# Half of x0 by a casting DMA, gated weights, x5 to x7 transposed by DMA, and state weights on 128x32 tiles in a fused attention and token-mixing kernel

## The chip, the cores and the metric

The kernel runs on one core of one Trainium2 chip. The metric is the device time of one execution in microseconds (us), lower is better. Executions fall into a fast and a slow state (of the changed kernel's five runs, 92.04 to 92.69 us against 93.85 and 94.79); all comparisons below are of fast runs, and where a profile was taken in a slow run this is said. The engines are PE (TensorE, matmuls), PEld (its weight loads), DVE (VectorE), ACT (ScalarE), POOL (GpSimd) and SP (here only a DMA issuer).

## The reference

Two layers. The first is a cross attention both ways between x (8 batches, 8 heads, 512 tokens, 64 values) and a state of 32 rows per head; the second mixes tokens with weights made from the tokens themselves.

```python
def _attn_ref(x, state):                       # x: 8,8,512,64; state: 8,8,32,64
    scores = scale * x @ state.T               # softmax, then xread = a @ state
    scores2 = scale * state @ x.T              # softmax, then sread = a2 @ x
    return np.concatenate([xread, sread], axis=2)
# ... heads are joined: 8, 544, 512
def _moe_ref(x, w_q, w_k, w_out):
    wq, wk = x @ w_q, x @ w_k                  # 64 wide
    W_tok = scale * np.einsum('bsd,btd->bst', wq, wk)
    mixed = np.einsum('bst,btd->bsd', W_tok, x)
    return np.maximum(mixed, 0) @ w_out
```

## The kernel before

One string, ORDER, lists every step as name.batch.form; a loop issues them in that order, and the trace has each engine's own in it (ACT: xc1.0 at 4.25 us, stf.0 at 6.00, xTe0.0 at 8.34). Forms: "t" is a matmul over the whole 128x128 array, "c" splits the output rows in two 64-column tiles (twice the instructions), a/v/p name ACT, DVE or POOL, "r" marks a step of fixed form. The data comes in as f32, and PE works in bf16. Batch 0 is loaded as f32 and cast on the engines; the others are cast by the DMA that POOL issues.

```python
ORDER = """
zst.0.p ix1.0.p stc.0.v xc1.0.a fill.1.t stt.0.c ste.0.v stbd.0.p stf.0.a xc0.0.p xc3.0.v ix2.0.p
fill.7.t xT0.0.t xc2.0.v xTe0.0.a fill.1.t xT1.0.t is.0.p ...
"""                                             # ... cut
    st_load(0, 1)                               # state of batch 0, f32, SP
    for g in range(4):                          # x0 in four f32 loads
        eng = nc.sync if g % 2 == 0 else nc.scalar
        eng.dma_start(out=x_f0[:, 2 * g : 2 * g + 2], in_=xsrc(0, 2 * g, 2 * g + 2))
    st_load(1, 3)
    for t in range(2):                          # w_q, w_k: four loads, no gate
        for r in range(2):
            nc.sync.dma_start(out=w_f[64 * r : 64 * r + 64, :, t, :], in_=wsrc[t][r])
    # ...
    def fill(n, b, e):                          # dummy matmuls that keep PE busy
        ps = psA.tile([128, 512], FP, name="fill_ps", tag="psA")
        for w in range(b):
            nc.tensor.matmul(out=ps, lhsT=zero[:, 0:128], rhs=zero, start=True, stop=True)
    def load(n, b, e):                          # ix1..ix7: f32 to bf16 by DMA
        nc.gpsimd.dma_start(out=x_bf[b], in_=xsrc(b, 0, H))          # cut
    def zeros(n, b, e):
        nc.gpsimd.memset(stT.bitcast(FP), 0.0)
    def sw_mm(n, p, e):                         # state weights: state @ w_q, w_k
        # for bb, q, r:
        nc.tensor.matmul(out=ps[NS * q : NS * q + NS, r, ...],
            lhsT=stT[64 * r : 64 * r + 64, 2 * p + bb, r, NP * r + q, :],
            rhs=w_qk[64 * r : 64 * r + 64, q, 0:2, :], start=True, stop=True)
    def xT_mm(n, b, e):                         # half a batch of x transposed on PE
        for q in range(NP):
            for u in range(2):
                tr(e, ps[:, u, q, :], x_bf[b][:, NP * r + q, 128 * u : 128 * u + 128])
    def x_dT(n, b, e):                          # defined, not used before
        xT = work.tile([128, H, 2, 128], BF, name="xTd", bufs=3)
        nc.sync.dma_start(out=xT.rearrange("p h u t -> p (h u) t"),
            in_=x_bf[b].rearrange("p h f -> p (h f)"), transpose=True)
        for r in range(2):
            L[b][f"xTe{r}"] = xT[:, NP * r : NP * r + NP].rearrange("p q u t -> p u q t")
```

Of each batch the steps are: xT (transpose x), pt (scores), exp, sums and srd (state read), wq/wk/g/v (small products), mix, fin (output product with w_out), os (store). fs and fix are the last output products.

The softmax here doesn't subtract the row's maximum and nothing guards it: scores larger than these inputs give would overflow.

## Time and profile before

| before | value |
|---|---|
| time, median of the runs beside the changed kernel | 88.26 us (87.6 to 88.69) |
| span of the profiled run, mean granted clock | 87.0 us, 0.991 |
| packets under 512 B, of all packets | 3712 of 15119 |
| x transposes on PE | 16 half batches |

How to read it: a page gives each engine's busy share, a row of tenths of busy time for 40 slices, the DMA queues and the chain of work that ended last. The prediction below shows those parts. Here are lines that it does not show: the DMA queues of the page (packets, MB, share of the 16 engines' span), then the view of the weights' tile, and two lines of the timeline (start us, length us, what).

```profile
q1 hardware_dynamic: 4880, 8.98, 28.0%
...
q8 instruction: 12, 0.20, 0.9%
```

```profile
L123 SPq DMA_DIRECT2D w_f<-in_moe_w_k_dram x2: 595/605/615, 4.2 to 4.9; - x2
L142 ACT CAST w_qk<-w_f x1: 620/620/620, 11.1 to 11.1; 128x512 bf16<-128x512 f32 x1
...
DMA to landing us min/median/max: 4.8/5.8/6.4
```

```profile
1.25 1.80 POOL L201 MEMSET stT<- 128x2048 f32 x1
...
3.67 0.41 DVE L144 CAST st_bf<-st_f 128x128 bf16<-128x128 f32 x1 [2.07 <-DMA st_f<-in_state_dram]
```

To see there: the weights are issued by 4.9 us and cast at 11.1, well ahead of their first use at 13.7 us. POOL's memset of stT is over (1.25 + 1.80) before DVE's first cast starts.

### The profile page before, as it was taken

How to read it: one execution, taken by the hardware profiler on the slowest of the kernel's cores; microseconds unless marked ns; L12 is line 12 of the kernel's file. 1: busy time of each engine (PE TensorE's matmuls, PEld its weight loads, DVE VectorE, ACT ScalarE, POOL GpSimd, SP SyncE). 2: the span in 40 equal slices, each digit the busy share in tenths (PEclk: the TensorE clock that was granted, in tenths of full speed). 3: DMA queues.
4: the chain of work that ended last, by engine and by line, in shares of the span. 5: the costliest groups of instructions: out<-in, count | busy, mean ns of one | idle time of the engine just before them, and what ended most of it. 6: DMA issues, size and time to landing. Idle time of an engine off the chain costs nothing.

```text
span 87.0 us, 3553 instructions
## 1 busy us (share of the span) xinstructions
PE 80.8 (93%) x1572; PEld 53.4 (61%) x1579; DVE 52.4 (60%) x111; ACT 55.9 (64%) x83; POOL 45.1 (52%) x58
## 2 busy tenths in 40 slices
PE   4999999999999999999999999999999999999910
PEld 1326666878777778777689747866755565544400
DVE  2125793997956875897856957891688264056010
ACT  1541637999898858778797838967930592665530
POOL 7999948999999969408507735327150000000000
PEclk9999999999999999999999999999999999999996
DMA  0899999999609999995600464201461663566782
GB/s 12 292 312 187 202 191 198 195 165 147 96 0 121 143 128 277 322 169 72 241 8 4 171 281 175 115 8 53 188 243 45 275 281 136 213 269 277 294 314 80
DMA packets 15119, 15.00 MB, mean 172 GB/s; under 512 B 3712, under 2 KB 12672, under 8 KB 15104
## 3 DMA queue, kind: packets, MB, share of 16 engines
q0 software_dynamic: 9104, 4.36, 39.7%
q1 hardware_dynamic: 4880, 8.98, 28.0%
q10 hardware_dynamic: 1120, 1.44, 4.6%
q8 instruction: 12, 0.20, 0.9%
q14 instruction: 3, 0.02, 0.1%
HBM read 10.22 MB, written 8.91 MB: 220 GB/s over the span
## 4 chain that ended last, share of the span: by engine, by line
PE 90%; ACT 4%; issue 1%; DVE 1%
PE fin_ps L161 20%; PE fin_ps L163 12%; PE fill_ps L155 6%; PE xT_ps L174 5%; PE mix_ps L541 5%; PE warm_ps L132 4%; PE srd_ps L369 3%; PE xT_ps L170 3%; PE at_ps L174 3%; PE v_ps L505 3%; PE pt_ps L163 2%; PE g_ps L163 2%; PE fins_ps L163 2%; PE wq_ps L433 2%; PE v_ps L514 2%; PE wk_ps L163 2%
## 5 line engine op out<-in xcount | busy, mean ns | idle before, releaser
L346 POOL TENSOR_TENSOR A<-E,rinv 128x1024 bf16<-128x1024 bf16 (+1 forms) x9 | 15.4, 1717 | 12.8 <-DVE rinv L340 12.5
L161 PE MATMUL fin_ps<-w_o,rmix 128*64 128x512 bf16 x160 | 19.4, 380 | 0.0
L142 ACT COPY ost<-fin_ps 128x1024 f32<-128x1024 f32 (+2 forms) x13 | 11.2, 864 | 11.6 <-PE fin_ps L161 5.9
L148 ACT ACTIVATE rmix<-mix_ps 128x1024 bf16<-128x1024 f32 x12 | 12.1, 1024 | 2.4 <-PE mix_ps L541 2.4
L407 POOL TENSOR_TENSOR sbd<-srn,mask 128x256 bf16<-128x256 bf16 x16 | 9.4, 614 | 6.0 <-DVE srn L397 5.9
L144 DVE COPY ost<-fin_ps 128x1024 f32<-128x1024 f32 (+1 forms) x6 | 6.5, 1091 | 9.9 <-PE fin_ps L163 5.4
L161 PEld LDWEIGHTS <-rmix 128*64 128x64 bf16 x160 | 8.4, 110 | 6.2 <-issue 0.6
L332 DVE TENSOR_REDUCE rsum<-E 128x16 f32<-128x512 bf16 x16 | 10.8, 676 | 0.9 <-ACT E L317 0.6
L163 PE MATMUL fin_ps<-w_o,rmix 128*128 128x512 bf16 x44 | 11.0, 379 | 0.2
L317 ACT ACTIVATE E<-pt_ps 128x512 bf16<-128x512 f32 x16 | 9.5, 601 | 2.5 <-PE pt_ps L161 1.3
L142 ACT COPY xT<-xT_ps 128x1024 bf16<-128x1024 bf16 x7 | 7.1, 1012 | 4.6 <-PE xT_ps L174 3.9
L234 POOL TENSOR_TENSOR stbd<-st_bf,mask 128x256 bf16<-128x256 bf16 x16 | 9.3, 610 | 0.4 <-DVE st_bf L144 0.2
L155 PE MATMUL fill_ps<-zero 128*128 128x512 bf16 x21 | 7.8, 432 | 0.1
L144 DVE COPY xT<-xT_ps 128x1024 bf16<-128x1024 bf16 x9 | 6.2, 690 | 2.7 <-PE xT_ps L174 2.5
L150 DVE TENSOR_SCALAR rmix<-mix_ps 128x1024 bf16<-128x1024 f32 x4 | 4.9, 1222 | 3.4 <-PE mix_ps L541 3.4
L163 PEld LDWEIGHTS <-rmix 128*128 128x128 bf16 x48 | 4.3, 98 | 4.0 <-ACT rmix L148 0.2
L183 POOL DMA_DIRECT2D x_bf<-in_x_dram x7 | 6.6, 949 | 0.0
L174 PE MATMUL xT_ps<-ident,x_bf 128*128 128x128 bf16 x80 | 6.0, 219 | 0.2 <-ACT E L317 0.2
L174 PEld LDWEIGHTS <-x_bf 128*128 128x128 bf16 x80 | 5.1, 98 | 1.3 <-issue 0.5
L541 PE MATMUL mix_ps<-wq,V 64*128 64x256 bf16 x64 | 5.8, 272 | 0.0
L132 PE MATMUL warm_ps<-zero 128*128 128x512 bf16 x8 | 3.6, 631 | 1.2 <-DVE mask L133 1.2
L163 PE MATMUL pt_ps<-stT,xT 128*128 128x64 bf16 x88 | 4.4, 193 | 0.0
(90 smaller groups left out, 139.7 us busy)
## 6 DMA issues: line engine op xcount, KB each, us to landing
out_dram<-ost SPq DMA_DIRECT2D x14, 512.0 KB, 2.8
x_bf<-in_x_dram POOLq DMA_DIRECT2D x7, 512.0 KB, 7.8
out_dram<-ost ACTq DMA_DIRECT2D x3, 256.0 KB, 2.1
x_f<-in_x_dram ACTq DMA_DIRECT2D x2, 256.0 KB, 4.0
x_f<-in_x_dram SPq DMA_DIRECT2D x2, 256.0 KB, 4.4
w_o<-in_moe_w_out_dram POOLq DMA_DIRECT2D x1, 512.0 KB, 8.4
out_dram<-ost SPq DMA_DIRECT2D x2, 256.0 KB, 2.4
st_bf<-in_state_dram POOLq DMA_DIRECT2D x1, 160.0 KB, 7.8
```

Source lines behind the costliest of these rows:

```text
L142: nc.scalar.copy(out=out, in_=in_)
L144: nc.vector.tensor_copy(out=out, in_=in_)
L148: nc.scalar.activation(out=out, in_=in_, func=AF.Relu)
L155: nc.tensor.matmul(out=ps, lhsT=zero[:, 0:128], rhs=zero, start=True, stop=True)
L161: nc.tensor.matmul(out=out[64 * h : 64 * h + 64], lhsT=lh, rhs=rhs, **kw)
L163: nc.tensor.matmul(out=out, lhsT=lhsT, rhs=rhs, **kw)
L174: nc.tensor.transpose(out=out, in_=in_, identity=ident)
L317: nc.scalar.activation(out=L[b]["E"][:, r].rearrange("p c q n -> p c (q n)"), in_=L[b][f"pt{r}"], func=AF.Exp, scale=float(scale),)
L332: nc.vector.reduce_sum(out=L[b]["rsum"][:, w], in_=L[b]["E"].rearrange("p r c q n -> p (r c q) n")[:, w], axis=AX.X,)
L346: eng.tensor_tensor(out=L[b]["A"].rearrange("p r c q n -> p (r c q) n")[:, w], in0=L[b]["E"].rearrange("p r c q n -> p (r c q) n")[:, w], ...
L407: nc.gpsimd.tensor_tensor(out=L[b]["sbd"][:, r], in0=L[b]["srn"][:, r : r + 1, :].to_broadcast((128, NP, D)), in1=mask[:, :, None].to_broa ...
L541: nc.tensor.matmul(out=ps[:, h, kk, :], lhsT=L[b]["V"][rows, 128 * k : 128 * k + 128], rhs=L[b]["wq"][rows, 0:SH], start=True, stop=True,)
```

## The change

The intent: take work off PE, the full engine. Batches 5, 6 and 7 are transposed by a DMA (xs steps, issued on SP; DMA_TRANSPOSE in the trace, called crossbar transposes here). Half of x0 comes in by a casting DMA that is issued first on POOL, and the weight loads wait for the first state cast (the gate: two tiny memsets of w_f on DVE stand behind that cast, at 5.26 us in the trace of after, and the loads follow them at 5.37; before, they began at 2.77). The state weights use the whole 128 rows of the array on 32-column tiles, against zero rows in stT. The whole order of steps is new, with fewer fills.

```diff
-zst.0.p ix1.0.p stc.0.v xc1.0.a fill.1.t stt.0.c ste.0.v stbd.0.p stf.0.a xc0.0.p xc3.0.v ix2.0.p
-fill.7.t xT0.0.t xc2.0.v xTe0.0.a fill.1.t xT1.0.t is.0.p stc.1.v fill.1.t stt.1.c xTe1.0.v stbd.2.p
+ix1.0.p zst.0.p stc.0.v wl.0.v fill.1.t stt.0.c xc1.0.v ste.0.a stf.0.v stbd.0.p xc0.0.v ix2.0.p
+fill.5.t xT0.0.t fill.1.t xT1.0.t xTe0.0.v is.0.p xTe1.0.v fill.1.t pt0.0.t ix3.0.p exp0.0.a stc.1.v
 ... (cut; from further on:)
+rs.4.v wq.2.c wks.2.c wqe.2.a wk.2.t fin3.0.t rinv.4.v wke.2.a xs.5.s srn.3.v A.4.p g.2.t ve.1.v
+sbd.3.p ate.3.v xs.6.s wq.4.c oe0.1.a wks.4.c stbd.6.p wq.3.c wqe.4.v wks.3.c mix1.2.r wqe.3.a
+wke.3.v fin2.1.t exp1.5.a ge.4.v mxe0.2.v g.3.t sums.5.t srd.5.r fin3.1.c srn.5.v os1.0.s xs.7.s
-    x_f0 = const.tile([128, H, NC * D], FP, name="x_f0")
+    x_f0 = const.tile([128, 4, NC * D], FP, name="x_f0")
-    for g in range(4):
-        eng = nc.sync if g % 2 == 0 else nc.scalar
+    for g, eng in enumerate((nc.sync, nc.scalar)):
-    for t in range(2):
-        for r in range(2):
-            nc.sync.dma_start(out=w_f[64 * r : 64 * r + 64, :, t, :], in_=wsrc[t][r])
+    nc.gpsimd.dma_start(out=x_bf[0][:, 4:H], in_=xsrc(0, 4, H))
+    nc.vector.memset(stT[:, 0].bitcast(FP), 0.0)
     def zeros(n, b, e):
-        nc.gpsimd.memset(stT.bitcast(FP), 0.0)
+        nc.gpsimd.memset(stT[:, 1:B].bitcast(FP), 0.0)
+    def w_load(n, b, e):                        # step wl, after the first state cast
+        nc.vector.memset(w_f[:, 0, 0, 0:1], 0.0)
+        nc.vector.memset(w_f[:, 0, 1, 0:1], 0.0)
+        for t in range(2):
+            for r in range(2):
+                nc.sync.dma_start(out=w_f[64 * r : 64 * r + 64, :, t, :], in_=wsrc[t][r])
-                        lhsT=stT[64 * r : 64 * r + 64, 2 * p + bb, r, NP * r + q, :],
-                        rhs=w_qk[64 * r : 64 * r + 64, q, 0:2, :],
+                        lhsT=stT[:, 2 * p + bb, r, NP * r + q, :],
+                        rhs=w_qk[:, q, 0:2, :],
```

## The prediction

> **What bounds the kernel now.** I read three views of the kernel before. First the page: which engine is full, and whether it has holes.

> ```profile
> span 87.0 us, 3553 instructions
> ...
> PE 80.8 (93%) x1572; PEld 53.4 (61%) x1579; DVE 52.4 (60%) x111; ACT 55.9 (64%) x83; POOL 45.1 (52%) x58
> ...
> PE   4999999999999999999999999999999999999910
> ```

> TensorE is busy from the second slice to the last but two with no hole; no other engine passes 64%. A busy PE is not a PE at its peak, so I went next to the chain of waits that ended last, in order of time (start us, length us, what). There one group follows another at the rate at which TensorE takes them in.

> ```profile
> 4.79 0.43 PE fill_ps L155
> ...
> 5.57 2.29 PE fill_ps L155 x7
> ...
> 8.31 0.22 PE fill_ps L155
> ...
> 13.63 1.01 ACT xT L142
> 14.65 0.60 ACT E L317
> ...
> 19.27 0.24 PE sw_ps L246 x16
> 19.51 0.34 PE pt_ps L163 x8
> ...
> 41.00 0.33 PE mix_ps L541 x4
> 41.33 0.98 PE fin_ps L161 x8
> 42.31 0.45 PE xT_ps L170 x16
> 42.76 0.86 PE fin_ps L161 x8
> 43.62 0.25 PE pt_ps L161 x16
> ...
> 79.42 3.47 PE fin_ps L163 x16
> 82.92 0.44 DVE ost L144
> ```

> The reader is to see four things. The chain is almost all PE (90% of the span); the stretches where ACT carries it lie between 13.6 and 18.6 us. A set of transposes of one half batch of x costs 0.45 us of pure PE time (42.31). The same eight fin matmuls cost 0.98 us right after mix and 0.86 us after transposes with an equal tile: changing the tile of the array costs 0.12 us. The same shows at pt (0.34 after sw, where eight of them otherwise take 0.23), and at v and wq (0.34 against 0.22). I take 0.11 per change. Fills are dummy matmuls, 0.43 us on the cold clock and 0.22 us on the warm one. Last, the time from the final matmul (82.9) to the end of the span (87.0) is 4.1 us of eviction, store and finish, which the change does not touch.

> The third view is the DMA issues with their time to landing, because the change moves work there.

> ```profile
> x_bf<-in_x_dram POOLq DMA_DIRECT2D x7, 512.0 KB, 7.8
> ```

> A 512 KB load by casting DMA takes a median 7.8 us to land beside other traffic (5.7 to 10.0 by the view of that tile). The four weight loads take 4.8 to 6.4 us.

> [...]

> **The change part by part.** I counted tiles and changes of tile from the order of the steps in both kernels.

> 1. Transposes of x5, x6, x7 leave TensorE: six half batches (16 before, 10 after) x 0.45 = 2.7 us, all of it on the bounding engine. Their six PSUM copies leave too: three on ACT at 1.01 us and three on DVE at 0.69 us by the grouped rows. Those engines are not the bound, so this is slack only.
> 2. Fills: 23 before, 20 after, two of the three in the group ahead of the first transposes. 3 x 0.22 = 0.65 us. [...]
> 3. Changes of tile, from the new order and the new state weights together: 58 before, 46 after. 12 x 0.11 = 1.3 us. Almost all of it is the order: the new order with the old 64x32 tile would have 47. Only the last sw now sits beside srd, which has the same 128x32 tile.
> 4. State weights on 128x32 tiles: 16 matmuls of 128 columns. Before, they took 0.24 us less a change of 0.11, so 0.13 on eight tiles. With four tiles, 16/4 x 0.056 (one 128-column pass: 0.45 us over 8 transposes) = 0.22. That loses 0.1 x 4 = 0.4 us. [...] one memset of 128x256 on DVE comes in, early and hidden.
> 5. x0 and weights: two of the four f32 loads and two of the four casts go (ACT 0.62, POOL 0.61 us); one casting DMA is issued first on POOL. The first transposes wait in fact for fills (they start at 7.70, while the casts for them ended by 5.9), so the earlier data is worth only what step 2 counts. The weight loads start after the first state cast (3.67 + 0.41 = 4.1) instead of 2.8. Issued 0.6 us apart, the last leaves SP at about 6.2 and lands about 6 later, near 12.3. The cast before was at 11.1, so ACT may wait 1 us there; sw.0 needs it at about 13.4 by my count, so it is just hidden.

> Sum: 2.7 + 0.65 + 1.3 - 0.4 = 4.25 us.

> Given back, as estimates: 0.3 us at the start, because both first xT copies now sit on DVE one behind the other (2 x 0.69) while the chain to pt shrank by a fill; and 0.5 us at the end, where mix, its two evictions and three small relus now stand close together ahead of the last stage with only 0.86 us of fs to cover them. Net 3.5 us. 88.2 - 3.5 = 84.7.

> **The rivals.** (a) DMA transposes land late and TensorE waits for them at pt. Adding up POOL's queue, I get x5 issued near 23, landed near 31, and its pt due near 40; x6 landed near 36, due near 45; x7 landed near 42, due near 51. So each has about 9 us[...]. At 12 us for one, the first pt waits 3 us and the time is near 87.5. Against this: the lead is large, the later two would shift with the first, and the DMA row in that part of the page has holes (31% mean share from 40 to 60 us). [...] (b) ACT or DVE becomes the bound. Against it: both lose some 2 to 4 us of work. I give it little. (c) Start-up takes the gain: late weights or a late casting DMA leave TensorE waiting at 8 to 14 us. That would be 1 to 1.5 us, so 86. (d) The tile change is cheaper than I take it, or the 12 removed are ones that waits hid anyway: then 1.3 falls to about 0.5 and the time is 85.5.

> **Range and chances.** All four terms whole and nothing given back is 84.0; a little more if idle in the ACT-carried stretch (13.6 to 18.6) shrinks too, 83.2. Rivals (c) and (d) together end near 86.5. So 84.7, range 83.2 to 86.8. The 2% mark is 86.46. Faster by over 2%: 0.82; within 2%: 0.14; slower: 0.04.

> **What would show it.** Right: span near 83.5; xT groups on PE 40% fewer; the last matmul near 79.4; no wait of PE for a transposing DMA[...]; DVE and ACT lower; sw groups at about 0.22. Wrong: a hole in the PE row between 38 and 52 us (rival a); holes in the first 15 us with ACT waiting for w_f or PE for x_bf (c); a tail from fs to the end longer by over 1 us; or fin groups still at 0.98 as often as before (d).

## The result, and the profile after

The changed kernel took 92.69 us (median of 5 runs, 92.04 to 94.79; fast ones 92.04, 92.44, 92.69) against 88.26 us: it is slower. The ratio of fast runs is 1.0473, 95% interval 1.0395 to 1.0551. A ratio here is always the mean time of one kernel's fast runs over the mean of the other's fast runs of the same rounds, so it is not quite the ratio of the medians. The predicted range ended at 86.8 us.

The profile of after fell in a slow run (93.85 us, clock 0.990); a fast run of it, profiled later (g0 below), has holes in the same places, smaller, and a longer wait at the start:

```profile
PE sw_ps L250 <- ACT w_qk L139: 1.9, 1, 1.9
...
PE wq_ps L437 <- issue: 0.9, 1, 0.9
PE pt_ps L160 <- DMA xTd<-x_bf: 0.8, 1, 0.8
PE srd_ps L373 <- issue: 0.7, 1, 0.7
```

So the sizes of the single waits below are those of one slow run, and only their places are seen in g0 too. First the page of that run:

```profile
span 90.4 us, 3407 instructions
...
PE 78.5 (87%) x1508; PEld 51.8 (57%) x1508; DVE 52.1 (58%) x110; ACT 51.2 (57%) x75; POOL 45.2 (50%) x58
...
PE   4999993989999999962884999999999999979920
...
q1 hardware_dynamic: 10848, 10.29, 43.8%
```

PE lost 2.3 us of busy time (the prediction counted 4.25), yet the span grew by 3.4. The PE row, solid before, has a dent in slice 7 (13.6 to 15.8 us), a wide one in slices 18 to 22 (38 to 50 us) and a small one ahead of the tail. SP's queue sends 10848 packets and not 4880: the three transposes, three times 2048 packets of 256 B. The chain that ended last, from first to last, by its lines around the dents:

```profile
3.72 1.60 DVE st_bf L141
...
7.49 6.76 DMA w_f<-in_moe_w_k_dram
...
14.35 0.63 ACT w_qk L139
...
15.02 0.42 PE sw_ps L250 x16
...
32.00 12.47 DMA xTd<-x_bf
...
44.52 0.41 PE pt_ps L160 x8
...
46.90 0.25 PE srd_ps L373 x18
47.15 1.60 issue
48.76 0.30 PE srd_ps L373 x14
...
80.32 1.02 ACT ost L139
81.34 0.04 issue
81.38 0.41 PE mix_ps L545 x4
81.79 0.02 issue
81.81 1.03 ACT rmix L145
82.84 0.05 issue
82.89 3.64 PE fin_ps L160 x16
```

Before, PE carried this chain for 90% of the span; now it carries 55%, DMA 25%. There are three new things in it. The first state cast takes 1.60 us, and the weights behind it land at 14.25. A transposing DMA takes 12.47 us here. And a stretch called "issue", in which PE waits for nothing that the profile shows, breaks a run of identical matmuls after the eighteenth. The waits of PE name a second stretch like it:

```profile
PE wq_ps L437 <- issue: 2.3, 1, 2.3
PE srd_ps L373 <- issue: 1.6, 1, 1.6
PE sw_ps L250 <- ACT w_qk L139: 1.4, 1, 1.4
...
PE pt_ps L160 <- DMA xTd<-x_bf: 0.2, 1, 0.2
```

The transpose that the chain blames costs PE only 0.2 us of waiting by itself: the hole just before it hides its lateness. Both are close behind each other, so removing one must be expected to bare the other. The tile of the transposes:

```profile
L282 SPq DMA_TRANSPOSE xTd<-x_bf x3: 3211/4277/5017, 32.0 to 48.9; - x3
...
DMA to landing us min/median/max: 6.9/7.0/12.5
```

The start, in the timeline:

```profile
3.62 1.61 POOL L198 MEMSET stT<- 128x1792 f32 x1
3.72 1.60 DVE L141 CAST st_bf<-st_f 128x128 bf16<-128x128 f32 x1 [1.75 <-DMA st_f<-in_state_dram]
```

POOL now issues two casting loads ahead of its memset (half of x0, and x1, which stood behind it before; 0.9 us each), and this pushed the memset from 1.25 to 3.62 us, onto DVE's first cast, which takes 1.60 us in place of 0.41. The cast ends at 5.32, just after the memset (5.23); e3 below tests whether the one delays the other.

```
kernel  block   passed   fetch           waited  used up  went on  hole  in the queues ahead of it
before  1217    32.63    36.01 - 36.93   3.4     38.41    38.44    0.0   stores 877 KB, casting load 219 KB
after   1217    34.00    38.57 - 40.66   4.6     39.73    42.28    2.55  casting load of 431 KB, others
after   1473    42.28    46.38 - 47.35   4.1     46.96    48.76    1.80  casting load 492 KB, 912 transposing packets
```

A fetch itself takes 0.9 to 2.1 us here, and in after PE goes on 1.6 and 1.4 us after it ends. Before, the same fetch waits 3.4 us behind stores and a casting load, and arrives just in time. (The core's DMA engines, 16 on the page, with what is queued for them are called the rings below.)

This gives two theories to test. **Mine:** the crossbar transposes cost PE through DMA traffic, in two ways that stand behind each other: x5's lands late, and fetches come late. The start costs a further part. **Rivals:** the new order alone (its boundaries fall elsewhere) makes the fetch holes, with transposes innocent; or the start sets the loss and the middle only eats slack.

### The profile page after: what moved, and what is told of

It reads as the page before. It is cut to its first block, busy times and chain, and to the rows that moved or that the text cites. A ratio compares the mean times of both kernels' runs of the same rounds, so it can differ in the third digit from the quotient of the medians.

```text
span 90.4 us, 3407 instructions
## 1 busy us (share of the span) xinstructions
PE 78.5 (87%) x1508; PEld 51.8 (57%) x1508; DVE 52.1 (58%) x110; ACT 51.2 (57%) x75; POOL 45.2 (50%) x58
## 3 DMA queue, kind: packets, MB, share of 16 engines
q1 hardware_dynamic: 10848, 10.29, 43.8%
## 4 chain that ended last, share of the span: by engine, by line
PE 55%; DMA 25%; DVE 6%; ACT 6%; issue 3%; SPq 1%; ACTq 0%
PE fin_ps L158 20%; DMA xTd<-x_bf 14%; DMA w_f<-in_moe_w_k_dram 7%; PE fin_ps L160 7%; PE mix_ps L545 4%; DMA st_f<-in_state_dram 3%; PE xT_ps L171 3%; ACT ost L139 3%; PE srd_ps L373 2%; PE pt_ps L160 2%; DVE st_bf L141 2%; PE v_ps L509 2%; PE at_ps L167 1%; PE v_ps L518 1%; PE sw_ps L250 1%
## 5 line engine op out<-in xcount | busy, mean ns | idle before, releaser
L158 PE MATMUL fin_ps<-w_o,rmix 128*64 128x512 bf16 x184 | 22.7, 380 | 0.0
L139 ACT COPY ost<-fin_ps 128x1024 f32<-128x1024 f32 (+2 forms) x16 | 14.3, 892 | 13.9 <-PE fin_ps L158 6.5
L158 PEld LDWEIGHTS <-rmix 128*64 128x64 bf16 x184 | 10.5, 110 | 5.8 <-issue 0.2
L336 DVE TENSOR_REDUCE rsum<-E 128x16 f32<-128x512 bf16 (+1 forms) x11 | 10.1, 918 | 0.7 <-ACT E L321 0.7
L160 PE MATMUL fin_ps<-w_o,rmix 128*128 128x512 bf16 x36 | 8.8, 380 | 0.1
L147 DVE TENSOR_SCALAR rmix<-mix_ps 128x1024 bf16<-128x1024 f32 x6 | 7.3, 1225 | 1.1 <-PE mix_ps L545 1.1
L141 DVE COPY ost<-fin_ps 128x1024 f32<-128x1024 f32 (+1 forms) x3 | 2.9, 958 | 5.5 <-PE fin_ps L160 4.2
L437 PE MATMUL wq_ps<-AT,sw 128*64 128x256 bf16 x32 | 3.4, 274 | 2.3 <-issue 2.3
L141 DVE COPY xT<-xT_ps 128x1024 bf16<-128x1024 bf16 x6 | 4.1, 690 | 1.5 <-PE xT_ps L171 1.4
L373 PE MATMUL srd_ps<-x_bf,E 128*32 128x64 bf16 x256 | 3.6, 195 | 1.6 <-issue 1.6
## 6 DMA issues: line engine op xcount, KB each, us to landing
out_dram<-ost SPq DMA_DIRECT2D x14, 512.0 KB, 3.3
x_bf<-in_x_dram POOLq DMA_DIRECT2D x7, 512.0 KB, 8.3
w_o<-in_moe_w_out_dram POOLq DMA_DIRECT2D x1, 512.0 KB, 11.2
```

The lines of the kernel that those rows point to most:

```text
L139: nc.scalar.copy(out=out, in_=in_)
L141: nc.vector.tensor_copy(out=out, in_=in_)
L158: nc.tensor.matmul(out=out[64 * h : 64 * h + 64], lhsT=lh, rhs=rhs, **kw)
L160: nc.tensor.matmul(out=out, lhsT=lhsT, rhs=rhs, **kw)
L336: nc.vector.reduce_sum(out=L[b]["rsum"][:, w], in_=L[b]["E"].rearrange("p r c q n -> p (r c q) n")[:, w], axis=AX.X,)
```

## The experiments

All kernels gave correct results. "Before" was run beside each. The runs came in five jobs, not all on one chip, so ratios compare best within a job. e1, e2 and e3 undo one part of the change each; e5 measures a suspected cost by itself.

### Job 1: e1, transposes back on PE

```diff
+... fin0.1.c xT0.5.c xTe0.5.v xT1.5.c xTe1.5.a     (x6 after fin3.1.c, x7 after fin3.2.t alike)
-xs.5.s   -xs.6.s   -xs.7.s
```

> The changed kernel with x5 to x7 transposed on TensorE again, placed one to two fin groups ahead of their pt; all else kept. Theory (the DMA transposes cost the time between 39 and 49 us: two holes in PE without a named wait, 2.3 and 1.6 us, and a late first batch): both holes go, about 4.3 us come back and 2.7 us of transposes are added, so some 1.6 us under the changed kernel, 90.5 to 91.5, and ratio to before about 1.03. Rival (the holes come from the new order on PE, not from the transposes): holes stay and the time is about 95.

Measured: 95.14 us (94.71 to 95.5), ratio 1.0761 (1.0652 to 1.087). The rival's side: without a single transposing packet the kernel is even slower, and the hole at instruction 1473 is there, at another instruction (an xT), 1.75 us from 39.22 to 40.97; the fetch had waited 4.4 us behind a casting load of 510 KB.

```profile
40.97 0.75 PE L168 MATMUL xT_ps<-ident,x_bf 128*64 128x128 bf16 x20 [1.53 <-issue]
```

So the hole follows the instruction number, and casting loads are enough to make it. The time says less: 2.3 us of it are two waits that after does not have, 0.8 us at srT and 1.5 us at mix, and h3 and i2, with these transposes in the same places on PE, have them too.

### Job 1: e5, transposes issued but not read

The kernel e1 with the three xs steps issued as in after; nobody reads what they write.

```diff
-        for r in range(2):
-            L[b][f"xTe{r}"] = xT[:, NP * r : NP * r + NP].rearrange("p q u t -> p u q t")
```

> As e1, but the three DMA transposes are still issued at their places and nobody reads what they write; TensorE transposes x5 to x7 itself. Theory (the traffic of the transposes holds back the fetch of PE's instructions): the holes without a named wait are there though no data is waited for, 3 to 4 us in all, and the time is 3 to 4 us over e1. Rival (PE loses time only by waiting for the transposed data): no holes, the same time as e1 within 0.5 us.

Measured: 100.12 us (fast runs 98.98 and 98.77), ratio 1.1185 (1.1001 to 1.1368): 3.8 us over e1's fast runs, for data that nobody waits for.

```profile
PE xT_ps L168 <- issue: 3.4, 1, 3.4
```

The same fetch now waited 5.6 us, behind the load and 716 transposing packets, and the hole grew by 1.8 us to 3.57. The rest is clock: after the hole the granted PE clock is 0.50 from 43 to 46 us and 0.61 from 46 to 49, which costs 3 x 0.50 + 3 x 0.39 = 2.7 us. Together 4.5 us, which more than covers the 3.8. This hole was paid for twice.

### Job 1: e2, weights loaded at the start

```diff
-wl.0.v
+    for t in range(2):           # ahead of the casting half of x0, on SP, no gate
+        for r in range(2):
+            nc.sync.dma_start(out=w_f[64 * r : 64 * r + 64, :, t, :], in_=wsrc[t][r])
```

> The changed kernel with the four weight loads issued at the start, ahead of the gate, as in the kernel before. Theory (the gate made the weights late: ACT waited 3.2 us for them, PE 1.4 us at sw): both waits go and the time falls by 1.4 to 2.5 us, to about 90.5. Rival (early weights only push the x0 loads back by as much): same time within 0.5 us, with a later first transpose than 7.3 us.

Measured: 91.33 us (fast 90.62 to 91.47), ratio 1.0299 (1.0096 to 1.0501). PE's wait at sw is gone. In its place it waits 0.9 us for x1 (until 12.4 us): the weights now take 7.1 to 8.2 us to land, and x1's load lands at 12.3 us and not at 10.9. The first sw starts at 14.7, 0.3 us earlier than after. The start is a trade between loads, which was the rival.

### Job 1: e3, zeros on DVE

```diff
-zst.0.p
-    nc.vector.memset(stT[:, 0].bitcast(FP), 0.0)
+    nc.vector.memset(stT.bitcast(FP), 0.0)
```

> The changed kernel with all of the zeros of stT written by DVE at the start, none by POOL. Theory (the POOL memset that ran from 3.6 to 5.2 us beside the first casts slowed them: 1.60 us where it was 0.41 before, and 1.33 where it was 0.45): the first cast takes about 0.4 us, the weights are issued near 4.3 instead of 5.4 us, and the wait at sw shrinks by about 1 us: time down 0.7 to 1.1. Rival (the casts are slow because of the casting DMA issued first): the cast still takes over 1 us and the time stays.

Measured: 91.89 us (fast 90.58, 91.34), ratio 1.0289 (1.0094 to 1.0485). The state cast takes 0.16 us, so POOL's memset was the cause of its 1.60. But the weights, issued 1.4 us earlier, land at the same time (7.1 to 7.8 us after their issue, against 5.2 to 6.8 in after; w_qk is cast at 14.2 against 14.35), and sw starts at 14.9: the earlier cast did not bring them in sooner. No run of after itself was in this job, so I claim no gain for e2 or e3.

### Job 2: f1, both repairs of the start

```diff
 (e2 and e3 together)
```

> The changed kernel with both repairs of the start: the weights issued at once, and the zeros written by DVE. Theory (the slow casts and the gated weights are one loss: PE waits 1.4 us at sw and 1.3 us more up to the first fin): the two repairs together bring 1.5 to 2.7 us, ratio to before 1.015 to 1.03. Rival (either repair pushes x1 or the casting half of x0 back, so that PE waits for data instead): no better than each alone, ratio 1.03, with a wait of PE for x ahead of 13 us.

Measured: 91.52 us median; the fast runs are 90.60 and 90.51, mean 90.56, against 88.31 of the fast runs of before: 1.025 by my own division. A miss: no better than either alone. The two fetch holes stay at 1.3 us each, and PE waits 0.6 us for x1 in place of the weights.

### Job 2: f2, the fetch boundary moved in after

The first 14 fills are cut in four: the same columns, but 42 more matmuls, with their weight loads 84 instructions, all in the first 20 us. Each boundary then falls on work some 84 instructions earlier.

```diff
-            nc.tensor.matmul(out=ps, lhsT=zero[:, 0:128], rhs=zero, start=True, stop=True)
+            cut = 4 if G["fills"] <= 14 else 1
+            for c in range(cut):
+                z = slice(512 // cut * c, 512 // cut * (c + 1))
+                nc.tensor.matmul(out=ps[:, z], lhsT=zero[:, 0:128], rhs=zero[:, z], start=True, stop=True)
```

> The changed kernel with 14 of its fills cut into four matmuls of 128 columns each: the same TensorE time, 84 more instructions ahead of everything. Theory (the holes at PE's instructions 1473 and 1729 are waits for its instruction fetch, one block of 256 ahead, held up behind loads and transposes on the DMA rings): the holes leave the matmuls of wq.4 and srd.5 and, where there are any, they sit 84 instructions earlier in the work. The first one should vanish, as its fetch is asked for near 32 us ahead of the load of x6; then PE meets the late transposes of x5 instead, and the time falls by 1.5 to 2 us. Rival (PE waits there for something in the program): the holes stay at wq.4 and srd.5.

Measured: 91.93 us (fast 91.78 to 92.0), ratio 1.0401 (1.0316 to 1.0486). Both fetch holes are gone, and the time is not. The profile (a slow run, 94.36 us) shows what took their place:

```profile
PE pt_ps L164 <- DMA xTd<-x_bf: 5.1, 1, 5.1
...
PE sw_ps L254 <- ACT w_qk L139: 1.0, 1, 1.0
```

x5's transpose took 14.8 us to land, and PE, which now reached its pt early, waited 5.1 us for it; the clock was then 0.50 for three more us. This is the prediction's rival (a), behind the fetch hole all along.

### Job 2: f3, the same shift in before

```diff
 (f2's cut of the fills, in the kernel before)
```

> The kernel before with the same 84 instructions added. Theory (fetch): the kernel before had no hole only because its blocks fell well; now one is asked for near 37 us, inside the load of x7, and the next block is needed near 40.6: a hole of 1.5 to 2.7 us appears there and the time rises by as much, 89.5 to 91. Rival (the fetch plays no part): same time as before within 0.5 us, no hole.

Measured: 90.06 us (89.98 to 90.35), ratio 1.02 (1.013 to 1.027). The kernel before, which had no fetch hole, gets three small ones (0.35, 0.64 and 0.32 us from row to row). The time rose by 1.8 us (90.1 against 88.3), with no crossbar transpose in the kernel. In the profiles, set side by side load by load, PE is 1.2 us late at the end: 0.2 us from the cut fills and 1.0 from the three boundaries.

### Job 2: f4, x7 alone by DMA in before

```diff
-xT0.7.c xTe0.7.a ... xT1.7.c xTe1.7.a
+xs.7.s   (after os1.1.s; pt1.7, exp1.7 and rs1.7 moved next to pt0.7, exp0.7 and rs0.7)
```

> The kernel before with only x7 transposed by DMA (its pt moved next to each other at 56 us, 7 us after the transpose should have landed). Theory (a transpose costs through its traffic and its lateness): landed by 50 us nobody waits for it, 0.9 us of transposes leave PE, but the fetches during 42 to 49 us come later; time between 0.9 us faster and 1 us slower, and a hole if any is at a multiple of 256 instructions. Rival (DMA transposes are harmless once they have lead): 0.8 to 1.0 us faster, no hole.

Measured: 88.93 us, ratio 1.0074 (0.9992 to 1.0155). 32 matmuls and their weight loads leave, and nothing is won. The transpose landed in 6.7 us, in time; but the fetch of block 1729, passed at 43.03, waited 2.7 us behind some 1900 of its packets (no casting load was there), and PE stood from 46.34 to 48.37.

```profile
PE wk_ps L162 <- issue: 1.8, 1, 1.8
```

### Job 3: g0, control, and g1, f4 with boundaries moved the other way

g0 is after, unchanged. In g1 eleven steps of f4 between 37 and 46 us go from "c" to "t": the same products with 65 fewer matmuls and as many fewer weight loads.

```diff
-xT1.6.c sums.5.c fin3.1.c xT0.6.c pt1.6.c fin0.1.c fin0.2.c pt0.6.c srT.5.c at.5.c fin1.2.c
+xT1.6.t sums.5.t fin3.1.t xT0.6.t pt1.6.t fin0.1.t fin0.2.t pt0.6.t srT.5.t at.5.t fin1.2.t
```

> The changed kernel again, unchanged, so that the next two are compared with it on one chip. Ratio to before 1.04 to 1.055; holes at PE's instructions 1473 and 1729, 1.5 to 3 us each; the transpose of x5 lands 11 to 15 us after its issue.

> f4 (only x7 by DMA, in the kernel before) with eleven steps between 37 and 46 us on full 128-column tiles instead of 64-column pairs: 130 instructions fewer ahead of the block whose fetch stood behind the transpose, for two more changes of tile (0.2 us). Theory (f4 lost its 0.9 us and more to one late fetch): the hole of 2.0 us at instruction 1985 goes, and the kernel is 0.5 to 1.3 us faster than before: ratio 0.985 to 0.995. Rival (a DMA transpose slows more than the fetch): still no faster than before, ratio 1.0 to 1.01.

Measured: g0 92.1 us (fast 90.39, 91.35), ratio 1.0302 (1.02 to 1.0404). g1 87.85 us, six runs all fast, ratio 0.9957 (0.9897 to 1.0016). It has no hole, and its transpose landed in 4.4 us. This is the best kernel, 0.4% under before, not clear of noise and just outside the range of the theory.

### Job 3: g2, the tail

```diff
-fs.3.t  -fse.3.v                                   (in the middle)
+mse.4.a fs.3.t ... fse.7.a fse.3.v                 (between the last evictions, as in before)
```

> The changed kernel with the first state output (fs.3) moved back behind the last mix, where the kernel before has it. Theory (PE idles 0.8 us near 81 to 83 us, because nothing covers the eviction ahead of the last mix and the last relu): the end loses its holes and the time falls by 0.7 to 1.1 us against the changed kernel of this job. Rival (the evictions set the end and fs only delays them): same within 0.3 us.

Measured: 93.64 us (fast 92.25, 93.29), ratio 1.0518 (1.0412 to 1.0623). A miss in time. Nothing ahead of fs.3 was changed, and the hole at row 1473 is where it is in g0; but its fetch waited 6.1 us, so that the hole is 3.1 us, after which the clock is 0.64 over four us. One and the same place of the program thus lost 0.9 (g0) to 2.8 us (g2) by the waits. Of the tail the trace says something: PE's idle time there falls from 0.8 us (g0) to 0.2, but a wait of 0.5 us opens at mix near 57 us, where fs.3 had stood.

### Job 3: g3, four repairs at once

```diff
 (e2's early weights, x5 back on PE, g2's tail, f2's shift)
```

> The changed kernel with the repairs that the runs point to: weights issued at once, x5 transposed on TensorE, fs.3 at the end, and the 84 extra instructions that moved the fetch. Theory (start 1 to 1.5 us, late x5 4.9 less 0.9, end 0.9): 85.5 to 88, ratio to before 0.97 to 1.0, with at most one hole under 2 us. Rival (each repair uncovers the next wait, as the fetch hole hid the late transpose): over 89, with PE waiting for the transposes of x6 or x7 or for the fetch near 46 us.

Measured: 88.98 us (fast 88.62 to 88.98), ratio 1.0067 (0.9976 to 1.0158). It missed its range by a little and wins back about 2 us against g0 in the same job. No fetch hole; the transposes of x6 and x7 land in 7.8 us. PE waits 1.2 us for x1, 0.5 at mix near 53 us, where fs.3 had stood, and 0.2 in the tail.

### Job 4: the loss priced step by step on one chip

h0 is after. h1 has x5 on PE and the shift. h2 has in addition the start of before. h3 has x6 and x7 on PE too.

```diff
 h1: -xs.5.s, +xT0.5.c xTe0.5.v xT1.5.c xTe1.5.a after fin0.1.c, and f2's cut of the fills
 h2: h1, with the loads, memsets and first steps of before, up to xTe0.0.a
 h3: h2, with xT, xTe of x6 and x7 placed as in e1, and no xs
```

> The kernel after, unchanged: the control of this job. 90 to 92.5 us in its fast runs, 3 to 5% over before, two holes in PE's work between 39 and 49 us as in every profile of it.

> The middle repaired and nothing else: x5 transposed on PE as before (32 more PE instructions), fourteen fills cut in four (84 more) so that PE's fetches meet other traffic; the start of after. Theory (the middle, fetches and late transposes, costs 3 to 5 us, the start 1 to 2.5): 88 to 89.5 us in fast runs, 2 to 3 us under the control. Rival (what is lost in the middle is given back by slack later, the start sets the end): within 1 us of the control.

> h1 with the start of before as well: x0 in four f32 loads cast on the engines, weights loaded without a gate, zeros of stT on POOL ahead of everything. Theory (start worth 1 to 2.5 us): 86.5 to 88, the first state-weight product at 13.5 to 14 us and not 15. Rival (the start is only traded against a wait for x1 a little earlier, as in the run with early weights): within 0.5 us of h1.

> h2 with x6 and x7 transposed on PE too, so that only the order, the 32-column state products and the tail of after are left. Theory (48 more PE instructions than h2, near 1.8 us of PE work, no transposing traffic): 1 to 2.5 us over h2, 88 to 90. Rival (the transposes of x6 and x7 still cost what they save): the same as h2 within 0.7 us.

| kernel | fast runs, mean us | ratio to before (95%) | first fin at, us | last output products at, us |
|---|---|---|---|---|
| h0 | 92.65 | 1.0457 (1.0352 to 1.0561) | (slow profile) | (slow profile) |
| h1 | 88.93 | 1.0037 (0.9984 to 1.0089) | 27.4 | 79.6 |
| h2 | 88.82 | 1.0025 (0.9967 to 1.0083) | 26.4 | 78.7 |
| h3 | 92.11 | 1.038, my division | 25.9 | 82.5 |

The middle is worth 3.7 us: nine tenths of what after lost. The start is worth 1.0 us in the traces at the first fin, 0.5 in the spans and 0.1 in the time, so its worth stays between these; in h1's profile its wait is still there (first line below) and hardly costs. h3 is a miss, on the instructive side: x6 and x7 by crossbar save 3.3 us, more than the 1.8 that their PE work counts. In h3 PE waits 2.3 us at two places of the middle that are free in h2 (second fence), near where I put x7's transposes back, so part of the 3.3 may belong to my placing, or to the four PSUM copies more that ACT and DVE then make; no run tells them apart.

```profile
PE sw_ps L254 <- ACT w_qk L139: 1.6, 1, 1.6
```

```profile
PE mix_ps L552 <- ACT rmix L148: 1.5, 1, 1.5
...
PE srT_ps L174 <- DVE srn L408: 0.8, 1, 0.8
```

### Job 5: i1 and i2, the missing corners

```diff
 i1: h1 with whole fills (no shift)
 i2: e1 with the shift
```

> After with x5 transposed on PE (32 more PE instructions), fills not cut, start unchanged. Theory (both causes are needed for the repair: with the fills whole, the fetch at the boundary near 34 us still waits behind x6's casting load and leaves a hole of 1.5 us or more): 90 to 92 us in fast runs, ratio 1.015 to 1.035, against 1.0037 with the fills cut as well. Rival (x5's transpose was the whole cause, the fetches lose nothing without it): within 0.7% of the run with both, no hole over 0.5 us between 36 and 50 us.

> After with no crossbar transpose at all (as the first experiment) and the fills cut; start of after. Theory (the first experiment's hole of 1.75 us at the fetch boundary near 39 us goes): ratio 1.04 to 1.055 against 1.076 there; about 1 us over the run without transposes and with the start of before. Rival (the hole of the first experiment was no matter of where the boundary lies): 1.07 to 1.085.

Measured: i1 89.77 us, four fast runs, ratio 1.0166 (1.0106 to 1.0226), with one fetch hole left; i2 93.32 us, ratio 1.0535 (1.0475 to 1.0594).

```profile
PE xT_ps L167 <- issue: 1.4, 1, 1.4
```

That settles the middle (ratios to before, of five jobs):

| | fills whole | fills cut (boundaries moved) |
|---|---|---|
| x5, x6, x7 by DMA | 1.047, 1.030, 1.046 (after, g0, h0) | 1.040 (f2) |
| x6, x7 by DMA, x5 on PE | 1.017 (i1) | 1.004 (h1) |
| all on PE, order of after | 1.076 (e1) | 1.054 (i2) |

Moving the boundaries alone gains little where x5's late transpose waits behind the hole (first row). With x5 on PE it gains 1.3% and without any transpose 2.2%. x5 on PE is the larger part, 1.3 to 3% without the shift and 3.6% with it. The rival "the order's boundaries alone" explains a part, and "the start" next to none.

## Why the prediction was wrong

**Step 1, x5 to x7 off PE, 2.7 us: right in PE's work, wrong in the landing.** The step that failed is the landing time of one transpose: the prediction took it to be well inside the lead of about 9 us, and nothing in the trace of before, which has no DMA transpose, showed that. A transpose of 512 KB landed in 4.4 us (g1) or 6.7 us (f4) where it was the only one; in 5.6 to 10.0 us, mostly about 7, for x6 and x7; and in 12.5 us for x5 (10.8 to 14.8 in the other runs of after's own middle), which shares the rings with a store and x6's casting load: its first packet moved only 36.9 us into the run, 4.9 after its issue. Rival (a) was stated at 12 us, with 87.5 us and a hole between 38 and 52 us in the PE row. The hole came. I gave the rival little because each transpose has a lead of about 9 us; the lead was about right (issued at 32.0 us behind the store os0.0, which SP issued at 31.53; due near 40), and the landing took 12.5 us.

**What no step or rival held** is PE's own program: that in these traces its fetches wait in the rings behind data (3.4 to 4.6 us in the table above), one block ahead. It made the holes of 2.55 and 1.80 us in after's profile. Three things show it: the holes sit at fixed instruction numbers (e1, at another instruction), they move when 84 instructions are added (f2, f3), and transposes that nobody reads enlarge them (e5). The two causes overlap, so they cannot be added: f2 took away the one and paid for the other. Together they cost 3.7 us on one chip (h0 against h1).

**Step 2, fills: right.** The page's group of fills went from 7.8 us (x21, of 23 in the order) to 7.2 (x20), 0.6 where 0.65 was counted; two of the 23 have no record, so the fall is a little larger.

**Step 3, 12 tile changes fewer, 1.3 us: there in PE's rows, not in the time.** Counted in the matmul rows of the traces there are 58 changes before and 46 after. Each takes about 0.1 us over the usual spacing, by my working 5.0 us in all before and 4.0 to 4.2 after. No run isolates what this is worth in time. The order of after with all transposes on PE and the start of before (h3) is 3.4 us above before, where the count (0.65 - 0.4 for fills, 1.3, -0.4 for sw, less 0.5 for the tail) said 0.65 below it; 2.3 us of this are the waits at mix and srT.

**Step 4, sw on 128x32: right.** The group of 16 takes 0.35 to 0.42 us in after's chain (15.02, 23.88, 26.29) against 0.24 before: 0.11 to 0.18 more where 0.1 was counted.

**Step 5, the start, "so it is just hidden": wrong, and small.** The gate opened at 5.3 us, not 4.1, because the cast took 1.60 us beside the memset (0.16 without it, e3); the weights landed at 14.25, not 12.3, and PE waited 1.4 us. That is rival (c). But e3 freed the cast and e2 the weights, and each only showed the next late load; h2 prices the whole start at 0.1 us of time and 1.0 us in the trace.

**Given back at the end, 0.5 us: about right.** In the tail the last mix waits 0.5 us for an eviction of ost, and the output products 0.1 us for the relu of rmix (80.32 to 82.89 in the chain, where ACT carries 2.05 us): PE is idle for 0.6 us there (0.8 in g0), against 0.16 before.

**What stays open.** h2, with the middle and the start repaired, is at 88.8 us. By the prediction's terms, with x5's 0.9 us and the two front fills (0.4) back on PE, it should be near 86. Its page has PE busy for 78.7 us against 80.8 before, so most of the work did leave. But between its first and last matmul PE is idle for 2.4 us against 0.9 before (worked out from the rows): 0.8 of it is in the tail, the rest lies in many small waits. The cost of the 84 cut pieces is in the difference too, and no run splits it.

## What to carry to other kernels

Before moving work from a full engine to DMA, lay the new transfer beside everything else that is in the rings in that stretch, and take its landing time from there, not from a bandwidth: 512 KB in 256 B packets took 4.4 to 14.8 us here. Where a trace shows an unexplained stop of PE in the middle of a run of equal matmuls, look at which instruction number it is at and at the "instruction" queue: here traffic delayed the program too (a fetch waited up to 6.1 us, g2), and fewer and larger instructions or a moved boundary cured it (g1, h1); a boundary moved blindly made holes (f3). When two delays stand one behind the other, undo both together, or each will look innocent.

## What these traces showed of the hardware

- Instruction fetch: packets of 16 KB, with PE's holes 256 rows apart. A fetch begins, but for a few, only when the block before it is entered, it waits up to 6.1 us (g2) behind data in the rings (a 510 KB casting load in e1, some 1900 transposing packets in f4), and PE stood 0.3 (f3) to 3.57 us (e5) at a boundary.
- A DMA transpose of 512 KB landed once in 4.4 us (g1), otherwise in 5.6 to 10.0 us, and in 10.8 to 14.8 us beside a casting load and a store.
- The clock after a hole: holes of 3.1 us (g2), 3.57 us (e5) and 5.3 us (f2) were followed by a mean granted clock of 0.64 (42 to 46 us), 0.50 (43 to 46) and 0.50 (47 to 50); the one of 2.55 us in after by 1.00 (42 to 51). In one slow profile (h0), where PE waited 2.1 us at sw, the clock was 0.77 from 15 to 18 us and 0.66 from 18 to 21. So the length of one hole does not settle it, and no run here isolates what does.
- A change of tile took 0.11 to 0.12 us (in before, fin takes 0.98 us after mix and 0.86 after an equal tile).
